# Order of matmuls in a six-layer cross network: two column groups interleaved over four pairs of PSUM banks, remainder rows of neighbouring groups placed side by side

## Chip and metric

One core of a Trainium2 chip. The metric is device microseconds of one execution. "Before" is an already tuned kernel.

## The reference

```python
B, F, D, L = 1024, 26, 32, 6          # Din = 26*32 = 832 columns
def reference(x0, ws, bs):            # x0 [1024, 832], ws [6, 832, 832], bs [6, 832], all bf16
    x = x0
    for l in range(6):
        x = x0 * (x @ ws[l] + bs[l]) + x
    return x
```

832 = 6 x 128 + 64. Each layer therefore has six full blocks of 128 and a remainder of 64, both in the rows that are contracted and in the columns that come out.

## The kernel before: what matters here

The batch lies along the free dimension, in two halves `c` of 512. A "group" is one block of output columns `j` of one layer (`KT = 7` groups: six full blocks and the remainder columns `KFULL`). TensorE works one group at a time, and alternates between two pairs of PSUM banks (PSUM is the memory into which matmuls add up their results). The loop, shortened:

```python
for g, (l, j) in enumerate(groups):          # layers 0-4: j = 0..6; layer 5: 6, 0..5
    s = g % 2                                # two bank pairs
    if g >= 2: eng.wait_ge(sem_act, group_first_item[g - 1])   # group g-2 evicted
    for kt in range(KT):                     # 6 full row blocks, then the 64 remainder rows
        for c in range(NCH):
            if first_in_layer: eng.wait_ge(sem_dve, ...)       # x tile kt, c of the layer before
            ...
            # kt < KFULL : rows 0:128                                    -> shape 128 x 128
            # kt == KFULL: rows 0:64 for c = 0, rows 64:128 for c = 1    -> shape  64 x 128
            # j == KFULL : columns 0:64 for c = 0, 64:128 for c = 1      -> 128 x 64, and 64 x 64
            mm = eng.matmul(ps_y[s][c], lhsT=w_sb[rows, l, kt, cols], rhs=xin[...],
                            start=(kt == 0), stop=(kt == KT - 1), tile_position=(trow, tcol))
```

The 64-row matmuls of the two halves run next to each other in the array; so do the 64-column ones. Two such matmuls are called a pair below. ScalarE evicts each half, that is, copies it out of PSUM with the bias added, to `t_buf`; VectorE multiplies by x0 and adds x. The add of item f is issued after the multiply of item f + 1. In layer 5 each finished block, except 4 and 5, is transposed by DMA (issued by SyncE) and stored by GpSimd; blocks 4 and 5 are transposed on TensorE and stored at the very end by SyncE and ScalarE, 256 KB each.

## Time and profile before

| | before |
|---|---|
| time, first measurement | 139.18 us (138.56 to 139.33, 4 runs) |
| span of the profiled run | 137.5 us, granted TensorE clock 0.993 |
| layers 1 to 4, start to start | 19.86 us each |
| layer 5, start to its last pair of matmuls | 20.24 us |
| last pair to the end of the span | 7.53 us |

Starts are those of the first weight load of a layer in the trace. The lines of the page and the views on which the argument rests are in the prediction below. How to read them: in these traces a weight load (PEld) between matmuls of one shape runs hidden under the matmul before it, so its row in the timeline goes on without a break. Where the shape changes, the row breaks; the bracket at the end of a row gives the idle time before it. A stay in the 64-row shape is called a visit or a cluster below, the time from the last pair to the end of the span the tail, and the time that one matmul or one pair takes up, 0.216 us, a slot.

### The profile page before, as it was taken

Reading aid. Unit: us, or ns where it says so; the run is one execution under the profiler, and the core shown is the slowest. Engines: PE = TensorE matmul, PEld = TensorE weight load, DVE = VectorE, ACT = ScalarE, POOL = GpSimd, SP = SyncE. Lnnn points to the kernel's source line nnn. Section 1 sums busy time; section 2 is a strip of 40 time slices with the busy share of each in tenths; the row PEclk is TensorE's granted clock in tenths of the full one; section 3 lists DMA queues with packets and bytes.
Section 4 is the critical chain, followed back from the end, with each engine's and each line's share of the span. In section 5 each row is a group of like instructions: output and inputs, shape, how many; then the busy total and the mean of one; then the engine's idle time right before and its main releaser. Section 6 shows DMA issues by size and latency. Waiting matters only on the chain.

```text
span 137.5 us, 1881 instructions
## 1 busy us (share of the span) xinstructions
PE 128.2 (93%) x692; PEld 55.5 (40%) x704; DVE 61.7 (45%) x164; ACT 52.0 (38%) x82; POOL 5.8 (4%) x12
## 2 busy tenths in 40 slices
PE   5989999999999999999999999999999989999930
PEld 5973333334443343333443343434433334433410
DVE  0180345553455453454473444463445552554570
ACT  0006544353433353333443344424444333333440
POOL 3000000000000000000000000000000000031520
PEclk9999999999999999999999999999999999999997
DMA  3998760000930001910003900005600000256757
GB/s 91 348 218 280 218 216 0 0 0 5 290 144 2 0 0 21 374 45 0 0 0 90 343 1 5 0 0 173 261 0 0 0 7 0 38 114 153 177 142 214
DMA packets 17016, 13.65 MB, mean 99 GB/s; under 512 B 7242, under 2 KB 16720, under 8 KB 17008
## 3 DMA queue, kind: packets, MB, share of 16 engines
q1 hardware_dynamic: 14192, 10.83, 26.5%
q10 hardware_dynamic: 2416, 1.52, 4.0%
q0 software_dynamic: 400, 1.19, 3.0%
q8 instruction: 5, 0.08, 0.3%
q14 instruction: 3, 0.02, 0.1%
HBM read 10.66 MB, written 1.70 MB: 90 GB/s over the span
## 4 chain that ended last, share of the span: by engine, by line
PE 80%; DMA 7%; ACTq 3%; ACT 3%; DVE 2%; issue 2%; POOL 1%; SPq 0%; DVEq 0%
PE ps_y L466 80%; DMA x_nat<-in_x_dram 4%; DMA o_sb<-xT_b 3%; ACT t_buf L519 2%; DVE u_buf L564 1%; ACTq L263 1%; ACT L498 1%; POOL out_dram L303 1%; DVE xT_a L578 1%; ACTq L245 1%; ACTq L248 0%; ACTq L256 0%; ACTq L260 0%; ACT x0T L506 0%; SPq L278 0%
## 5 line engine op out<-in xcount | busy, mean ns | idle before, releaser
L519 ACT ACTIVATE t_buf<-ps_y,bias_T 128x512 bf16<-128x512 f32 x77 | 49.1, 683 | 69.0 <-PE ps_y L466 69.0
L564 DVE TENSOR_TENSOR u_buf<-t_buf,x0T 128x512 bf16<-128x512 bf16 x76 | 32.1, 422 | 64.4 <-ACT t_buf L519 64.4
L466 PE MATMUL ps_y<-xT_a,w_sb 128*128 128x512 bf16 (+3 forms) x288 | 59.8, 382 | 0.7 <-DVE xT_a L578 0.3
L466 PE MATMUL ps_y<-xT_b,w_sb 128*128 128x512 bf16 (+2 forms) x192 | 39.5, 382 | 0.3 <-issue 0.2
L466 PEld LDWEIGHTS ps_y<-xT_a,w_sb 128*128 128x128 bf16 (+3 forms) x294 | 23.6, 99 | 36.7 <-issue 13.2
L466 PEld LDWEIGHTS ps_y<-xT_b,w_sb 128*128 128x128 bf16 (+3 forms) x196 | 15.7, 99 | 24.1 <-issue 9.1
L466 PE MATMUL ps_y<-x0T,w_sb 128*128 128x512 bf16 (+3 forms) x96 | 19.7, 382 | 0.5 <-ACT x0T L506 0.3
L578 DVE TENSOR_TENSOR xT_b<-u_buf,xT_a 128x512 bf16<-128x512 bf16 x37 | 15.2, 417 | 0.0
L466 PEld LDWEIGHTS ps_y<-x0T,w_sb 128*128 128x128 bf16 (+3 forms) x98 | 7.8, 99 | 12.2 <-issue 3.9
L578 DVE TENSOR_TENSOR xT_a<-u_buf,xT_b 128x512 bf16<-128x512 bf16 x26 | 10.7, 418 | 0.0
L303 POOL DMA_DIRECT2D out_dram<-o_sb x5 | 4.5, 895 | 127.3 <-DMA o_sb<-xT_b 127.3
L498 ACT ACT_TABLE_LOAD x1 | 1.3, 1283 | 11.1 <-issue 11.1
L360 PE MATMUL ps_x<-ident 128*128 128x128 bf16 x36 | 4.0, 313 | 1.5 <-POOL ident L336 1.5
L578 DVE TENSOR_TENSOR xT_a<-u_buf,x0T 128x512 bf16<-128x512 bf16 x13 | 5.3, 417 | 0.0
L360 PEld LDWEIGHTS ps_x<-ident 128*128 128x128 bf16 x36 | 3.8, 149 | 1.5 <-POOL ident L336 1.5
L554 DVE COPY x0T<-ps_t 128x1024 bf16<-128x1024 bf16 x2 | 1.3, 686 | 6.3 <-PE ps_t L393 6.3
L554 DVE COPY x0T<-ps_y 128x1024 bf16<-128x1024 bf16 x4 | 2.6, 686 | 0.4 <-PE ps_y L393 0.3
L393 PE MATMUL ps_y<-ident,x_nat 128*128 128x128 bf16 x32 | 2.1, 220 | 0.5 <-DMA x_nat<-in_x_dram 0.5
L393 PEld LDWEIGHTS ps_y<-ident,x_nat 128*128 128x128 bf16 x32 | 1.8, 98 | 0.7 <-DMA x_nat<-in_x_dram 0.7
L484 PE MATMUL ps_t<-ident,xT_b 128*128 128x128 bf16 x8 | 0.8, 222 | 1.3 <-DVE xT_b L612 0.9
L393 PE MATMUL ps_t<-ident,x_nat 128*128 128x128 bf16 x16 | 1.3, 251 | 0.0
L393 PEld LDWEIGHTS ps_t<-ident,x_nat 128*128 128x128 bf16 x16 | 1.3, 120 | 0.0
(26 smaller groups left out, 10.1 us busy)
## 6 DMA issues: line engine op xcount, KB each, us to landing
w_sb<-in_ws_dram SPq DMA_DIRECT2D x10, 624.0 KB, 4.7
w_sb<-in_ws_dram SPq DMA_DIRECT2D x10, 104.0 KB, 5.1
x_nat<-in_x_dram SPq DMA_DIRECT2D x2, 512.0 KB, 4.6
out_dram<-o_sb POOLq DMA_DIRECT2D x4, 256.0 KB, 3.8
w_sb<-in_ws_dram ACTq DMA_DIRECT2D x1, 864.0 KB, 5.0
x_nat<-in_x_dram SPq DMA_DIRECT2D x1, 640.0 KB, 6.7
out_dram<-o_sb SPq DMA_DIRECT2D x1, 256.0 KB, 2.3
out_dram<-o_sb ACTq DMA_DIRECT2D x1, 256.0 KB, 2.6
```

Source lines behind the costliest of these rows:

```text
L245: eng.dma_start(w_sb[0:REM, 0, KFULL, c0:c1], ws[0, RB:D, c0:c1]).then_inc(sem_w0blk[j], 16)
L263: eng.dma_start(w_sb[REM : 2 * REM, 0, KFULL, c0:D], ws[0, RB:D, c0:D]).then_inc(sem_w[0], 16)
L303: eng.dma_start(out[:, c0:c1].rearrange("(bo bi) f -> bi bo f", bi=P), o_sb[:, :, c0:c1],).then_inc(sem_out, 16)
L360: eng.matmul(ps_x[:, 0:P], lhsT=ident[:, :], rhs=ident[:, :], start=True, stop=True)
L393: eng.matmul(pt[:, bt * P : (bt + 1) * P], lhsT=x0_nat[:, bt, kt * P : (kt + 1) * P], rhs=ident[:, :], is_transpose=True,).then_inc(sem_tr, 1)
L466: mm = eng.matmul(o_ap, lhsT=lhsT, rhs=rhs, start=(kt == kt_first), stop=(kt == kt_last), tile_position=(trow, tcol), skip_group_check=(tc ...
L484: eng.matmul(pt[:, bb * P : (bb + 1) * P], lhsT=xf[:, j, bt * P : (bt + 1) * P], rhs=ident[:, :], is_transpose=True,).then_inc(sem_otr, 1)
L498: eng.activation(bias_T[:, 0:NB_COLS], ps_x[:, 0:NB_COLS], ACT_F.Copy).then_inc(sem_bc, 1)
L519: eng.activation(t_buf[:, slot, :], src, ACT_F.Identity, bias=bias_col(l, j), scale=1.0,).then_inc(sem_act, 1)
L554: eng.tensor_copy(x0T[:, kt, 0:ncol], tr_bank[kt][:, 0:ncol]).then_inc(sem_cp_v, 1)
L564: eng.tensor_tensor(u_buf[:, us, :], t_buf[:, slot, :], x0T[rows, tile, cols], ALU.mult,).then_inc(sem_u, 1)
L578: eng.tensor_tensor(xout[rows, tile, cols], u_buf[:, us, :], xin[rows, tile, cols], ALU.add,).then_inc(sem_dve, 1)
```

## The change

Its intent: fewer changes between full and 64-row matmuls, more slack in PSUM, and no start of a layer with a short group. It has four parts, in the diff as follows.

```diff
+ # (1) "SG": two groups interleaved, kt outermost; (2) third field 1: remainder rows first
+        if l == 0:
+            ph = [("G", [0]), ("G", [1], 1), ("SG", [2, 3]), ("SG", [4, 5]), ("G", [KFULL])]
+        elif l < L - 1:
+            ph = [("SG", [0, 1]), ("SG", [2, 3], 1), ("SG", [4, 5]), ("G", [KFULL])]
+        else:                       # (4) remainder columns no longer first in layer 5
+            ph = [("SG", [0, 1]), ("G", [KFULL]), ("G", [2], 1), ("G", [3])]
+            ph += [("G", [4], 1), ("G", [5])]
-        order = list(range(KT)) if l < L - 1 else [KFULL] + list(range(KFULL))
 ...
-        ps_y = [[ps_y0, ps_y1], [ps_y2, ps_y3]]
+        BP = [(ps_t0, ps_t1), (ps_y0, ps_y1), (ps_y2, ps_y3), (ps_b, ps_x)]   # (3), bitcasts cut
+        def bank_pair(g): return BP[g % NBP]
 ...
-                if g >= 2:
-                    eng.wait_ge(sem_act, group_first_item[g - 1])
+                if g >= NBP:
+                    eng.wait_ge(sem_act, group_first_item[g - NBP + 1])
 ...
+                        ktl = list(range(KT)) if not rem_first else [KFULL] + list(range(KFULL))
+                        for kt in ktl:
+                            for g, j in zip(gs, js):
+                                for c in range(NCH):
+                                    mm = eng.matmul(...)
 ...
+                    if l == L - 1 and (j, c) in [(KFULL, None)]:
+                        emit_add(f)         # VectorE: no deferral for the remainder columns
```

More of the change, by code (lines that the diff above doesn't have):

```diff
@@ L35, in bass_standalone__dcn_v2_cross__recsys_kernel @@
     UB_R = 4
+    SGW = 2
+    assert KFULL % SGW == 0
+    layer_phases = []
+    for l in range(L):
+        if l == 0:
[5 more added lines that the diff above has]
+            ph += [("G", [4], 1), ("G", [5])]
+        ph = [(p + (0,))[:3] for p in ph]
+        layer_phases.append(ph)
     groups = []
     for l in range(L):
-        order = list(range(KT)) if l < L - 1 else [KFULL] + list(range(KFULL))
-        for j in order:
-            groups.append((l, j))
+        for kind, js, _rf in layer_phases[l]:
+            for j in js:
+                groups.append((l, j))
     NG = len(groups)
@@ L58, in bass_standalone__dcn_v2_cross__recsys_kernel @@
     group_first_item.append(NF)
-    layer_first_item = [group_first_item[group_pos[(l, (0 if l < L - 1 else KFULL))]] for l in range(L)]
+    layer_first_item = [group_first_item[l * KT] for l in range(L)]
     layer_first_item.append(NF)
@@ L139, in bass_standalone__dcn_v2_cross__recsys_kernel @@
         block = es.enter_context(nc.Block(no_gpsimd_drain=True))
-        ps_y = [[ps_y0, ps_y1], [ps_y2, ps_y3]]
-        ps_t = [ps_t0, ps_t1]
         xT_bufs = [xT_a, xT_b]
@@ L166, in bass_standalone__dcn_v2_cross__recsys_kernel, with bank_pair @@
                 cp_wait.append((False, n_cp_v))
-        assert NPE == 2
-        s_last = (NG - 1) % 2
+        BP = [
+            (ps_t0[:, :].bitcast(FP32), ps_t1[:, :].bitcast(FP32)),
+            (ps_y0[:, :], ps_y1[:, :]),
+            (ps_y2[:, :], ps_y3[:, :]),
+            (ps_b[:, :], ps_x[:, :]),
+        ]
+        NBP = len(BP)
+        def bank_pair(g):
+            return BP[g % NBP]
+        assert NPE == 2 and NBP >= 4
         def piece_psum(k, c):
             if k == len(pe_groups) - 1:
-                return ps_t[c][:, 0 : HBT * P]
-            return ps_y[1 - s_last][c][:, :].bitcast(BF16)[:, 0 : HBT * P]
+                return bank_pair(NG - 3)[c].bitcast(BF16)[:, 0 : HBT * P]
+            return bank_pair(NG - 2)[c].bitcast(BF16)[:, 0 : HBT * P]
         def final_store(eng, c, sem):
@@ L416, in wait_x0T_copy @@
                 eng.wait_ge(sem_cp_a if on_act else sem_cp_v, cnt)
-            tr_bank_users_g0 = [kt for kt in range(KT) if tr_bank[kt].tensor.name in ("ps_y0", "ps_y1")]
-            for g, (l, j) in enumerate(groups):
-                xin = x_in(l)
-                s = g % 2
-                first_in_layer = group_first_item[g] == layer_first_item[l]
-                if g >= 2:
-                    eng.wait_ge(sem_act, group_first_item[g - 1])
-                kt_order = list(range(KT))
-                kt_first, kt_last = kt_order[0], kt_order[-1]
-                if True:
-                    for kt in kt_order:
-                        for c in range(NCH):
-                            if first_in_layer:
-                                if l == 0:
-                                    if c == 0:
-                                        if kt == kt_first:
-                                            for ku in tr_bank_users_g0:
-                                                wait_x0T_copy(ku)
-                                        wait_x0T_copy(kt)
-                                else:
-                                    eng.wait_ge(sem_dve, item_index[(l - 1, kt, c)] + 1)
-                                if kt == kt_first and c == 0 and l > 0:
-                                    eng.wait_ge(sem_w[l], W_SEM_TOTAL)
-                            if l == 0 and kt == kt_first and c == 0:
-                                if j < W0_NBLK:
-                                    eng.wait_ge(sem_w0blk[j], W0_BLK_TOTAL)
-                                elif j == W0_NBLK:
-                                    eng.wait_ge(sem_w[0], W0_REST_TOTAL)
-                            if kt < KFULL:
-                                rows = slice(0, P)
-                                rhs = xin[:, kt, c * NW : (c + 1) * NW]
-                                trow = 0
-                            elif c == 0:
-                                rows = slice(0, REM)
-                                rhs = xin[0:REM, KFULL, 0:NW]
-                                trow = 0
-                            else:
-                                rows = slice(REM, 2 * REM)
-                                rhs = xin[REM : 2 * REM, KFULL, 0:NW]
-                                trow = REM
-                            if j < KFULL:
-                                lhsT = w_sb[rows, l, kt, j * P : (j + 1) * P]
-                                o_ap = ps_y[s][c][:, :]
-                                tcol = 0
-                            else:
-                                lhsT = w_sb[rows, l, kt, RB:D]
-                                o_ap = ps_y[s][0][c * REM : (c + 1) * REM, :]
-                                tcol = c * REM
-                            mm = eng.matmul(
-                                o_ap,
-                                lhsT=lhsT,
-                                rhs=rhs,
-                                start=(kt == kt_first),
-                                stop=(kt == kt_last),
-                                tile_position=(trow, tcol),
-                                skip_group_check=(tcol != 0),
-                            )
-                            if kt == kt_last and (j < KFULL or c == NCH - 1):
-                                mm.then_inc(sem_mm, 1)
@@ new lines, in _, with pre_group_waits @@
+            tr_bank_names = [tr_bank[kt].tensor.name for kt in range(KT)]
+            def pre_group_waits(g):
+                l, j = groups[g]
+                if g >= NBP:
+                    eng.wait_ge(sem_act, group_first_item[g - NBP + 1])
+                else:
+                    for bnk in bank_pair(g):
+                        name = bnk.tensor.name
+                        for kt in range(KT):
+                            if tr_bank_names[kt] == name:
+                                wait_x0T_copy(kt)
+                        if name == "ps_x":
+                            eng.wait_ge(sem_bc, 1)
@@ new lines, in mm_operands @@
+            def mm_operands(l, j, kt, c, g):
+                xin = x_in(l)
+                if kt < KFULL:
+                    rows = slice(0, P)
+                    rhs = xin[:, kt, c * NW : (c + 1) * NW]
+                    trow = 0
+                elif c == 0:
+                    rows = slice(0, REM)
+                    rhs = xin[0:REM, KFULL, 0:NW]
+                    trow = 0
+                else:
+                    rows = slice(REM, 2 * REM)
+                    rhs = xin[REM : 2 * REM, KFULL, 0:NW]
+                    trow = REM
+                if j < KFULL:
+                    lhsT = w_sb[rows, l, kt, j * P : (j + 1) * P]
+                    o_ap = bank_pair(g)[c]
+                    tcol = 0
+                else:
+                    lhsT = w_sb[rows, l, kt, RB:D]
+                    o_ap = bank_pair(g)[0][c * REM : (c + 1) * REM, :]
+                    tcol = c * REM
+                return o_ap, lhsT, rhs, trow, tcol
@@ new lines, in tile_wait, with weights_wait @@
+            def tile_wait(l, kt, c):
+                if l == 0:
+                    wait_x0T_copy(kt)
+                else:
+                    eng.wait_ge(sem_dve, item_index[(l - 1, kt, c)] + 1)
+            def weights_wait(l, js):
+                if l > 0:
+                    eng.wait_ge(sem_w[l], W_SEM_TOTAL)
+                else:
+                    for j in js:
+                        if j < W0_NBLK:
+                            eng.wait_ge(sem_w0blk[j], W0_BLK_TOTAL)
+                    if max(js) >= W0_NBLK:
+                        eng.wait_ge(sem_w[0], W0_REST_TOTAL)
@@ new lines, in _ @@
+            for l in range(L):
+                first_phase = True
+                for kind, js, rem_first in layer_phases[l]:
+                    gs = [group_pos[(l, j)] for j in js]
+                    if kind == "G":
+                        g = gs[0]
+                        j = js[0]
+                        pre_group_waits(g)
+                        ktl = list(range(KT)) if not rem_first else [KFULL] + list(range(KFULL))
+                        for kt in ktl:
+                            for c in range(NCH):
+                                if first_phase:
+                                    if kt == KFULL or j == KFULL:
+                                        if c == 0:
+                                            for cc in range(NCH):
+                                                tile_wait(l, kt, cc)
+                                    else:
+                                        tile_wait(l, kt, c)
+                                if kt == ktl[0] and c == 0 and (first_phase or l == 0):
+                                    weights_wait(l, js)
+                                o_ap, lhsT, rhs, trow, tcol = mm_operands(l, j, kt, c, g)
+                                mm = eng.matmul(
+                                    o_ap,
+                                    lhsT=lhsT,
+                                    rhs=rhs,
+                                    start=(kt == ktl[0]),
+                                    stop=(kt == ktl[-1]),
+                                    tile_position=(trow, tcol),
+                                    skip_group_check=True,
+                                )
+                                if kt == ktl[-1] and (j < KFULL or c == NCH - 1):
+                                    mm.then_inc(sem_mm, 1)
+                    else:
+                        assert all(j < KFULL for j in js)
+                        for g in gs:
+                            pre_group_waits(g)
+                        assert not (first_phase and rem_first)
+                        if l == 0 and rem_first:
+                            weights_wait(l, js)
+                        ktl = list(range(KT)) if not rem_first else [KFULL] + list(range(KFULL))
+                        for kt in ktl:
+                            if first_phase:
+                                for cc in range(NCH):
+                                    tile_wait(l, kt, cc)
+                            if kt == 0 and (first_phase or l == 0) and not rem_first:
+                                weights_wait(l, js)
+                            for g, j in zip(gs, js):
+                                for c in range(NCH):
+                                    o_ap, lhsT, rhs, trow, tcol = mm_operands(l, j, kt, c, g)
+                                    mm = eng.matmul(
+                                        o_ap,
+                                        lhsT=lhsT,
+                                        rhs=rhs,
+                                        start=(kt == ktl[0]),
+                                        stop=(kt == ktl[-1]),
+                                        tile_position=(trow, tcol),
+                                        skip_group_check=True,
+                                    )
+                                    if kt == ktl[-1]:
+                                        mm.then_inc(sem_mm, 1)
+                    first_phase = False
@@ L512, in _ @@
                 g = group_pos[(l, j)]
-                s = g % 2
                 slot = f % TB_R
@@ L517, in _ @@
                 eng.wait_ge(sem_mm, f + 1)
-                src = ps_y[s][c][:, :] if j < KFULL else ps_y[s][0][:, :]
+                src = bank_pair(g)[c] if j < KFULL else bank_pair(g)[0]
                 eng.activation(
@@ L589, in _ @@
                     f1 = NF - 2
+                pend = None
                 for f in range(f0, f1):
                     emit_mult(f)
-                    if f > f0:
-                        emit_add(f - 1)
-                emit_add(f1 - 1)
+                    if pend is not None:
+                        emit_add(pend)
+                    pend = f
+                    _, j, c = items[f]
+                    if l == L - 1 and (j, c) in [(KFULL, None)]:
+                        emit_add(f)
+                        pend = None
+                if pend is not None:
+                    emit_add(pend)
             xin5 = x_in(L - 1)
@@ L604, in _ @@
                 out=u_buf[:, us1, :],
-                in0=ps_y[s_last][1][:, :],
+                in0=bank_pair(NG - 1)[1],
                 scalar=bias_col(L - 1, J_LAST),
```

## The prediction

> **What bounds the kernel now.** I read the page first, then its chain of work, then the timeline of the weight loads (PEld).
>
> ```profile
> PE 128.2 (93%) x692; PEld 55.5 (40%) x704; DVE 61.7 (45%) x164; ACT 52.0 (38%) x82; POOL 5.8 (4%) x12
> ...
> PE   5989999999999999999999999999999989999930
> PEld 5973333334443343333443343434433334433410
> DVE  0180345553455453454473444463445552554570
> ...
> PE 80%; DMA 7%; ACTq 3%; ACT 3%; DVE 2%; issue 2%; POOL 1%; SPq 0%; DVEq 0%
> ```
>
> TensorE is busy from slice 3 to slice 37 and holds 80% of the chain that ended last; VectorE and ScalarE are under half busy. So there is next to no waiting to remove, and the question is whether a "busy" TensorE does useful work all the time. A busy digit can't tell, because modelled ends of matmuls overlap the next start. Starts can. A weight load that can't be hoisted stands within 4 ns of its matmul, so the PEld timeline marks the places where the array changes its shape; here it is in layer 0:
>
> ```profile
> 16.17 0.10 PEld L466 LDWEIGHTS ps_y<-x0T,w_sb 64*128 64x128 bf16 x2 [0.42 <-issue]
> 16.49 2.27 PEld L466 LDWEIGHTS ps_y<-x0T,w_sb 128*128 128x128 bf16 x12 [0.23 <-issue]
> 19.18 0.10 PEld L466 LDWEIGHTS ps_y<-x0T,w_sb 64*128 64x128 bf16 x2 [0.42 <-issue]
> 19.51 2.27 PEld L466 LDWEIGHTS ps_y<-x0T,w_sb 128*128 128x128 bf16 x12 [0.23 <-issue]
> 22.20 0.10 PEld L466 LDWEIGHTS ps_y<-x0T,w_sb 64*128 64x128 bf16 x2 [0.42 <-issue]
> ```
>
> One column group is twelve full matmuls (six row blocks, two batch halves) and one pair of 64-row matmuls for the remainder of 64 rows, which run side by side (their starts are 4 ns apart in the single records). The period is (22.20 - 16.17) / 2 = 3.015 us; 3.019 from the single matmul records. Full matmuls start every 0.216 us. Thirteen such slots are 2.807 us, so **0.21 us of each group is neither a matmul slot nor a wait**: it is the way into and out of the 64-row shape. From the starts of the single matmuls: the last full one to the 64-row pair 0.312 instead of 0.216 (0.096 extra); the pair to the next full one 0.323, and that one takes 0.226 (0.117 extra together). Measured in the same way at the end of each layer: 64-row pair to the 128x64 shape of the remainder columns 0.127 extra; 128x64 to 64x64 0.096; 64x64 back to full 0.129, or 0.142 where a 128x64 group follows (layer 4 to 5).
>
> Only one real wait stands in the matmul stream after layer 0 has begun, in the last layer, which begins with the short remainder-column group:
>
> ```profile
> 109.42 0.11 PEld L466 LDWEIGHTS ps_y<-xT_b,w_sb 64*64 64x64 bf16 x2 [0.41 <-issue]
> 109.75 1.00 PEld L466 LDWEIGHTS ps_y<-xT_a,w_sb 128*64 128x64 bf16 x11 [0.23 <-issue]
> 111.53 0.11 PEld L466 LDWEIGHTS ps_y<-xT_a,w_sb 128*64 128x64 bf16 x1 [0.77 <-DVE xT_a L578]
> 111.86 0.11 PEld L466 LDWEIGHTS ps_y<-xT_a,w_sb 64*64 64x64 bf16 x2 [0.23 <-DVE xT_a L578]
> 112.20 0.55 PEld L466 LDWEIGHTS ps_y<-xT_a,w_sb 128*128 128x128 bf16 x4 [0.23 <-issue]
> ```
>
> This group takes 112.20 - 109.75 = 2.45 us; the same group in the other layers takes 1.75 (48.42 to 50.17 in the same view). So 0.70 us is waiting for VectorE's add on the previous layer's last tiles. In the other layers no first group waits (30.316 to 33.335 is again 3.019); the 0.4 us holes that the chain shows there, such as 41.33 to 41.76, are records that are missing, since the count of twelve comes out one short each time.
>
> The end, from the chain in order of time:
>
> ```profile
> 128.25 0.42 DVE u_buf L564
> 128.67 0.11 DVE xT_b L578
> 128.78 0.14 issue
> 128.92 0.11 DVE u_buf L564
> 129.03 3.99 DMA o_sb<-xT_b
> 133.02 0.28 issue
> 133.31 0.89 POOL out_dram L303
> ```
>
> The last matmul pair starts at 129.99; the span ends 7.5 us later. Bound there is not that pair's own output (its store has landed at 136.17) but column block 3: its last add waits, by program order, behind the first multiply of block 4, then transposes by DMA, then is stored and lands at 137.13.
>
> **What the Trainium skill says.** "TensorEngine Tiling (Array Packing)", Key Properties: "Changing tiling mode (not just tile) drains the TensorE". The trace agrees, at 0.10 to 0.14 us a change. "TensorE: Matmul & The Clock Gate", the section on 56 ns against 53.3: a warm matmul of 512 columns takes 512/2.4 GHz plus about 2.5 ns, 215.7 ns; the trace has 216, so no slot can become shorter. The same page, The mechanism: a weight load overlaps running matmuls only when its row group differs. The trace shows more: in the 128x128 and 128x64 shapes loads of about 0.1 us are hidden and slots stay at 0.216 and 0.216. For two 64-row pairs in succession, which the change makes for the first time, no run shows it. "TensorEngine Tiling", Gotcha 1: row tiles must not be in the same PSUM bank at once; the two halves of a pair keep separate banks in the change.
>
> **The change part by part.** It (1) handles two column groups together, row block outermost; (2) lets alternate phases begin with the remainder rows, so that their 64-row pairs touch those that ended the phase before; (3) uses four pairs of PSUM banks in place of two, which (1) and (2) need; (4) in layer 5 puts blocks 0 and 1 ahead of the remainder columns. Matmul slots, evictions, VectorE work and bytes stay the same in number. Weight loads too: each matmul keeps its own, hidden as now.
>
> Shape changes before. Layers 0 to 3: five inner clusters at 0.096 + 0.117 = 0.213, the sixth into the remainder columns 0.096 + 0.127, then 0.096 + 0.129: 1.065 + 0.223 + 0.225 = 1.513 us. Layer 4: 1.526. Layer 5: 0.225 + 1.065 + 0.096 = 1.386. In all 4 x 1.513 + 1.526 + 1.386 = 8.96 us.
>
> After. Layer 0: clusters {block 0, block 1} and {2, 3} at 0.213, {4, 5} 0.223, remainder columns 0.225: 0.874. Layers 1 to 4: one inner cluster {0, 1, 2, 3}, {4, 5} at 0.223, 0.225: 0.661 each. Layer 5: {0, 1} into the remainder columns 0.223, into 64x64 0.096, from there into block 2's 64-row pair about 0.12 (not seen so far; an estimate between the 0.096 and 0.142 above), out 0.117, {3, 4} 0.213, into block 5's pair 0.096: 0.865. In all 0.874 + 4 x 0.661 + 0.865 = 4.38 us. **Gain 4.58 us**, all of it in TensorE's stream, so on the path.
>
> The wait in layer 5: 5.4 us of work on blocks 0 and 1 now hide the adds: block 5's tiles are needed 20 slots (4.3 us) into the layer instead of 1.1. Gain 0.70 us.
>
> The end: block 4 now ends with full matmuls and its first half is out earlier, 2.64 instead of 2.53 us before the last pair's start, which brings block 3's add 0.1 us forward against the end. The rest stays: 0.1 us. At the head nothing moves: the first group still waits 0.32 us at its remainder pair (13.15) for ScalarE's copy, and the weights of block 1 (landed 10.34, now wanted 13.37) and of the rest (landed 14.27, wanted 16.28) are there.
>
> Sum: 4.58 + 0.70 + 0.1 = 5.4 us; 139.18 - 5.4 = **133.8 us**.
>
> **The rivals.** (a) *Bunched results make new waits.* Four halves now finish within 0.43 us instead of two. ScalarE issues evictions 0.585 us apart, VectorE two operations at 0.336 each, so a bunch of four is through about 4 us after its first pair starts. Next layer's first phase needs block 4's banks free 2.29 us after that start (two pairs' slots, then 1.75 of remainder columns) and has them at 0.485 + 0.585 + 0.68 = 1.75; it needs block 5's tiles at 6.6 and has them at about 4.6. It fits, by 0.5 and 2 us. Were it to miss by 0.5 us at five boundaries: 136.3. Chance about 7%. (b) *The second 64-row pair's load is not hidden.* Then each of the 21 pairs that now follow another pair costs some 0.1 us again: 2.1 us, 135.9. The 128x64 shape, where loads are hidden, speaks against it. Chance about 10%. (c) *The end takes back the gain*: the DMA transposes of blocks 2 and 3 come 2.7 instead of 3.0 us apart and share the queues with stores; a transpose took 3.0 to 4.0 us in this trace. Half a us either way. (d) Weights of the next layer are asked for after 5.6 instead of 3.0 us of a layer and land 6.7 us later, well within 19 us: hidden as now.
>
> **Range and chances.** The middle is the sum. Downwards only the end (a 3 us transpose) and the unseen shape change move it: 133.0. Upwards rival (c), some of (a) or half of (b): 135.4. Two per cent faster is 136.4; (a) or (b) alone stay under it, both together pass it. Faster 0.93, same 0.06, slower 0.01.
>
> **What would show it.** Right: PEld timeline of layers 1 to 4 with two 64-row clusters per layer instead of six, of eight and four loads; layers of 19.0 us instead of 19.86; pairs inside a cluster 0.216 apart (0.31 would be rival b); no wait on VectorE at layer 5's start; a tail after the last pair still of 7.4 us. Wrong: waits of TensorE on ScalarE or VectorE at layer starts, or a clock granted lower than the present 0.993.

## The result

| | before | after |
|---|---|---|
| time, median | 139.0 us (138.46 to 139.48, 16 runs) | 133.9 us (133.22 to 134.52, 11 runs) |
| ratio | | 0.963, 95% interval 0.9609 to 0.9651 |
| profiled span | 137.5 us | 131.5 us |
| layers 0, 1 to 4, 5 | 20.18, 4 x 19.86, 20.24 | 19.22, 4 x 19.01, 19.01 |
| last pair to the end | 7.53 us | 7.55 us |

A ratio is the mean time of one kernel's runs over the mean of the other's of the same rounds, so it is not quite the ratio of the medians. The two profiled spans differ by 6.0 us, the medians by 5.1. The profiled execution before was one of its slower ones: layer 0 waited 0.32 us there for a copy, and began 0.44 us later than in the profile after. In the run of this kernel with earlier adds (below), whose head is the same, layer 0 took 19.86. With that value the matmul stream from the start of layer 0 to the last pair is 5 x 19.86 + 20.24 = 119.54 before and 19.22 + 5 x 19.01 = 114.27 after: 5.27 us less.

The page of the changed kernel:

```profile
PE 123.0 (93%) x692; PEld 55.8 (42%) x704; DVE 59.9 (46%) x164; ACT 49.7 (38%) x82; POOL 5.8 (4%) x12
...
PE   5989999999999999999999999999999999999920
...
DVE  0280433556166274338091628190725370934660
ACT  0006515171427090616170724451642623534430
```

TensorE has the same number of matmuls and the same busy share; the share says nothing of the gain. VectorE and ScalarE were level before; now they swing between 0 and 9 tenths, since results come four halves at a time. TensorE does not wait for them: from the start of layer 0 to the last pair the totals of its waits name neither.

The timeline of weight loads after, from the start of layer 1 to that of layer 2; it answers to the one of layer 0 in the prediction:

```profile
28.91 0.10 PEld L543 LDWEIGHTS ps_b<-xT_a,w_sb 128*128 128x128 bf16 x1 [0.23 <-issue]
...
34.20 0.09 PEld L543 LDWEIGHTS ps_b<-xT_a,w_sb 64*128 64x128 bf16 x1 [0.42 <-issue]
34.20 0.09 PEld L543 LDWEIGHTS ps_x<-xT_a,w_sb 64*128 64x128 bf16 x1
34.21 0.10 PEld L543 LDWEIGHTS ps_t<-xT_a,w_sb 64*128 64x128 bf16 x2
34.43 0.31 PEld L543 LDWEIGHTS ps_y<-xT_a,w_sb 64*128 64x128 bf16 x4
35.17 4.86 PEld L543 LDWEIGHTS ps_y<-xT_a,w_sb 128*128 128x128 bf16 x24 [0.42 <-issue]
...
45.63 0.09 PEld L543 LDWEIGHTS ps_b<-xT_a,w_sb 64*128 64x128 bf16 x1 [0.42 <-issue]
...
46.17 1.00 PEld L515 LDWEIGHTS ps_y<-xT_a,w_sb 128*64 128x64 bf16 x12 [0.42 <-issue]
...
47.92 0.11 PEld L543 LDWEIGHTS ps_y<-xT_b,w_sb 128*128 128x128 bf16 x2 [0.23 <-issue]
```

Eight 64-row loads stand together at 34.20, and the next full load comes at 35.17: four pairs for one visit to the 64-row shape. The second cluster, at 45.63, serves blocks 4 and 5. There are two visits in a layer where there were six, and the layer takes 47.92 - 28.91 = 19.01 us.

The start of layer 5, which answers to the lines with the wait for VectorE:

```profile
110.25 0.10 PEld L543 LDWEIGHTS ps_t<-xT_a,w_sb 64*128 64x128 bf16 x2
110.78 1.00 PEld L515 LDWEIGHTS ps_y<-xT_a,w_sb 128*64 128x64 bf16 x12 [0.42 <-issue]
112.19 0.11 PEld L515 LDWEIGHTS ps_y<-xT_a,w_sb 64*64 64x64 bf16 x2 [0.41 <-issue]
112.53 0.10 PEld L515 LDWEIGHTS ps_y<-xT_a,w_sb 64*128 64x128 bf16 x2 [0.23 <-issue]
112.85 0.55 PEld L515 LDWEIGHTS ps_y<-xT_a,w_sb 128*128 128x128 bf16 x4 [0.23 <-issue]
```

All idle time here ends by "issue", none by VectorE. The remainder columns take 112.53 - 110.78 = 1.75 us, as in any other layer.

The end did not go as predicted. The transfers by kind in the last part of the trace (operation, count, KB each, median us from issue to landing), before:

```profile
out_dram<-o_sb SPq DMA_DIRECT2D x1, 256.0 KB, 2.3
out_dram<-o_sb ACTq DMA_DIRECT2D x1, 256.0 KB, 2.6
```

and after:

```profile
out_dram<-o_sb SPq DMA_DIRECT2D x1, 256.0 KB, 3.3
out_dram<-o_sb ACTq DMA_DIRECT2D x1, 256.0 KB, 3.5
```

The last of the chain is now ScalarE's store, not GpSimd's. Block 3's transpose took 3.08 us instead of 3.99, so its store was issued 2.3 us after the last pair instead of 3.3. It then ran ahead of the two final stores, which landed 1.0 and 0.9 us later after the last pair than before.

### The profile page after: what moved, and what is told of

Read it like the earlier page. It is cut to its first block, busy times and chain, and to the rows that moved or that the text cites. A ratio compares the mean times of both kernels' runs of the same rounds, so it can differ in the third digit from the quotient of the medians.

```text
span 131.5 us, 1929 instructions
## 1 busy us (share of the span) xinstructions
PE 123.0 (93%) x692; PEld 55.8 (42%) x704; DVE 59.9 (46%) x164; ACT 49.7 (38%) x82; POOL 5.8 (4%) x12
## 4 chain that ended last, share of the span: by engine, by line
PE 86%; DMA 5%; DVE 3%; issue 1%; SPq 1%; ACT 1%; DVEq 0%; ACTq 0%
PE ps_y L543 30%; PE ps_t L543 17%; PE ps_y L515 11%; PE ps_b L543 9%; PE ps_x L543 8%; PE ps_t L515 6%; DMA x_nat<-in_x_dram 5%; PE ps_b L515 2%; PE ps_x L515 1%; DVE u_buf L641 1%; PE ps_y L414 1%; SPq L299 1%; DVE u_buf L687 1%; ACT t_buf L596 1%; DVE xT_b L655 0%
## 5 line engine op out<-in xcount | busy, mean ns | idle before, releaser
L596 ACT ACTIVATE t_buf<-ps_y,bias_T 128x512 bf16<-128x512 f32 x37 | 23.2, 689 | 31.8 <-PE ps_y L543 23.9
L543 PE MATMUL ps_y<-xT_b,w_sb 128*128 128x512 bf16 (+1 forms) x81 | 22.8, 379 | 0.2
L596 ACT ACTIVATE t_buf<-ps_t,bias_T 128x512 bf16<-128x512 f32 x21 | 13.4, 688 | 16.9 <-PE ps_t L543 14.6
L543 PE MATMUL ps_y<-xT_a,w_sb 128*128 128x512 bf16 (+1 forms) x81 | 17.3, 379 | 0.2
L543 PE MATMUL ps_t<-xT_a,w_sb 128*128 128x512 bf16 (+1 forms) x54 | 15.4, 379 | 0.1
L543 PE MATMUL ps_t<-xT_b,w_sb 128*128 128x512 bf16 (+1 forms) x41 | 11.7, 380 | 0.1
L543 PE MATMUL ps_b<-xT_a,w_sb 128*128 128x512 bf16 (+1 forms) x28 | 10.7, 381 | 0.0
L543 PE MATMUL ps_x<-xT_a,w_sb 128*128 128x512 bf16 (+1 forms) x28 | 10.6, 380 | 0.0
L515 PE MATMUL ps_y<-xT_a,w_sb 128*64 128x512 bf16 (+3 forms) x56 | 9.7, 383 | 0.0
L543 PE MATMUL ps_b<-xT_b,w_sb 128*128 128x512 bf16 (+1 forms) x21 | 8.0, 379 | 0.0
```

Of the source, the lines that this page charges most:

```text
L515: mm = eng.matmul(o_ap, lhsT=lhsT, rhs=rhs, start=(kt == ktl[0]), stop=(kt == ktl[-1]), tile_position=(trow, tcol), skip_group_check=True,)
L543: mm = eng.matmul(o_ap, lhsT=lhsT, rhs=rhs, start=(kt == ktl[0]), stop=(kt == ktl[-1]), tile_position=(trow, tcol), skip_group_check=True,)
L596: eng.activation(t_buf[:, slot, :], src, ACT_F.Identity, bias=bias_col(l, j), scale=1.0,).then_inc(sem_act, 1)
```

## The experiments

Every experiment was timed in five rounds against the kernel before, whose median over these rounds was 138.82 to 138.85 us. "Layers" are read as in the table above. The diffs of the orders are put in short form. The runs with parts of the change are made from the changed kernel, so they keep the rest of its code too, such as the undeferred add of the remainder columns.

### Part 3 alone: four pairs of banks

```diff
+ ph = [("G", [j]) for j in order]     # order as before: 0..6; layer 5: 6, 0..5
```

> Part 3 alone: four pairs of PSUM banks, with the old order of groups and rows. My theory (the gain is fewer shape changes of the array plus one removed wait): the shape changes and the wait in layer 5 stay, so 139.0 us, within 0.3 of before, and layers of 19.86 us. Rival (TensorE was held back at group ends by PSUM banks that were not yet free): most of the gain of 5.1 us comes here, 134 to 136.

Measured: 138.94 us, ratio 1.0014 (0.9991 to 1.0038); layers 19.86, layer 5 20.33. No gain from banks: TensorE had not been waiting for them. That the other parts need the four pairs is argued from the code; none was run with two.

### Parts 3 and 4: order in layer 5

```diff
- layer 5: G 6, G 0, G 1, G 2, G 3, G 4, G 5
+ layer 5: G 0, G 1, G 6, G 2, G 3, G 4, G 5
```

> Parts 3 and 4: as the one before, and in layer 5 the remainder columns go behind blocks 0 and 1, one group at a time. My theory: only the wait of 0.70 us at the start of layer 5 goes and the number of shape changes stays: 138.3 us, with no wait on VectorE there. Rival (the wait is hidden by the tail, which ends later in any case): 139.0.

Measured: 137.94 us, ratio 0.9946 (0.9921 to 0.9971), 0.75 us less; layer 5 19.54, 0.70 less than before. The wait was on the path, and its worth is its length.

### Parts 2 and 3: neighbouring remainder rows without interleaving

```diff
+ layers 0-4: G 0, G 1 (rem first), G 2, G 3 (rem first), G 4, G 5 (rem first), G 6
+ layer 5:    G 6, G 0, G 1 (rem first), G 2, G 3 (rem first), G 4, G 5
```

> Parts 2 and 3 without interleaving: one group at a time, but blocks 1, 3, 5 (1 and 3 in layer 5) begin with the remainder rows, so that 64-row pairs of two groups touch; layer 5 in the old order. My theory: shape changes cost 0.98 us in layers 0 to 4 (three clusters at 0.213, full into 128x64 taken as 0.12, 0.225) and 0.96 in layer 5, 5.9 in place of 8.96; gain 3.0 us, the wait in layer 5 stays: 136.0 us, layers 1 to 3 of 19.3 us. Rival (the gain is interleaving of two groups, whatever it does for the array): 139.0.

Measured: 135.91 us, ratio 0.9794 (0.9767 to 0.982); layers 0 to 4 19.33. Six visits became three without any interleaving, and 2.9 us were gained. So the gain follows the number of shape changes. The new change from full straight to 128x64 fits the 0.12 that was taken for it: first steps of 0.309 and 0.237 us where 0.216 and 0.213 would be without it.

### Parts 1, 3 and 4: interleaving without neighbouring remainder rows

```diff
- ("G", [1], 1)   ("SG", [2, 3], 1)   ("G", [2], 1)   ("G", [4], 1)
+ ("G", [1])      ("SG", [2, 3])      ("G", [2])      ("G", [4])
```

> Parts 1, 3 and 4 without part 2: groups interleaved in twos as in the change, but every phase ends with its remainder rows. My theory: 1.087 us of shape changes in layer 0, 0.874 in layers 1 to 4, 1.18 in layer 5, 5.77 in place of 8.96, and the wait of 0.70 gone: gain 3.9 us, 135.1 us, layers 1 to 4 of 19.2 us, 1.3 us above the whole change. Rival (interleaving alone makes the gain): 133.9.

Measured: 135.02 us, ratio 0.9731 (0.9706 to 0.9756); layers 1 to 4 19.22. Interleaving is worth what it merges: two pairs per visit, three visits a layer.

### The change with part 4 undone

```diff
- layer 5: SG 0 1, G 6, G 2 (rem first), G 3, G 4 (rem first), G 5
+ layer 5: G 6, G 0, G 1 (rem first), G 2, G 3 (rem first), G 4, G 5
```

> The change with part 4 undone: layer 5 begins with the remainder columns again, then blocks 0 to 5 one at a time with 1 and 3 beginning with their remainder rows. My theory: the wait at the start of layer 5 comes back and is longer than the old 0.70 us, since layer 4 now hands over four halves at once: its last add is at about 5.05 us after the last 64-row cluster starts, and the 64x64 pair that needs it would be due at 3.7, so 1.4 us; and 0.1 us of shape changes: 1.5 us over the whole change, 135.4. Rival (the old wait of 0.70 simply comes back): 134.7.

Measured: 135.68 us, ratio 0.9768 (0.9735 to 0.9802); layer 5 20.61. The weight loads at the start of layer 5:

```profile
105.58 0.57 PEld L515 LDWEIGHTS ps_b<-xT_a,w_sb 128*64 128x64 bf16 x8 [0.23 <-issue]
106.78 0.14 PEld L515 LDWEIGHTS ps_b<-xT_a,w_sb 128*64 128x64 bf16 x2 [0.63 <-DVE xT_a L655]
108.12 0.14 PEld L515 LDWEIGHTS ps_b<-xT_a,w_sb 128*64 128x64 bf16 x2 [1.20 <-DVE xT_a L655]
...
108.83 0.11 PEld L515 LDWEIGHTS ps_t<-xT_a,w_sb 128*128 128x128 bf16 x2 [0.23 <-issue]
```

The remainder columns take 108.83 - 105.58 = 3.25 us instead of 1.75: a wait of 1.50 us, twice the old one, so the rival fell. The time itself is 1.8 us above the change's, but three of its six executions have 2.9 to 3.1 us between span and time, where nearly all others of this study have 1.7 to 2.1; by the spans (medians 133.35 and 131.85) it is 1.5 us, as expected. Interleaving at the end of a layer hands VectorE four halves at once, and a short group at the start of the next can't cover them. Parts 1 and 4 belong together.

### The price of a shape change, by taking the shape away

Wrong result on purpose (relative error 0.049): both halves' remainder rows are read by full-height matmuls.

```diff
-  elif c == 0: rows, rhs, trow = slice(0, REM), xin[0:REM, KFULL, 0:NW], 0
-  else:        rows, rhs, trow = slice(REM, 2*REM), xin[REM:2*REM, KFULL, 0:NW], REM
+  else:        rows, rhs, trow = slice(0, P), xin[:, KFULL, 0:NW], 0
```

> Wrong result on purpose. The kernel before, with the remainder rows done as two full 128-row matmuls one after the other (both halves' rows are read, so the sums are wrong) in place of one pair of 64-row ones side by side. A group then has 14 full slots and no shape change inside. My theory (0.21 us of each group is the change of shape): 14 x 0.216 = 3.02 us, as long as before, so 139.0 within 0.4 us although 36 more slots are used. Rival (the 0.21 us belongs to the end of a group, its semaphore or the change of PSUM banks): 3.23 us a group, 36 x 0.21 = 7.6 us more, 146.6.

Measured: 138.99 us, ratio 1.0015 (0.999 to 1.0039). Weight loads of layer 2 in this run:

```profile
50.38 17.81 PEld L462 LDWEIGHTS ps_y<-xT_b,w_sb 128*128 128x128 bf16 x84 [0.41 <-ACT t_buf L515]
68.61 1.22 PEld L462 LDWEIGHTS ps_y<-xT_b,w_sb 128*64 128x64 bf16 x14 [0.42 <-issue]
```

84 loads of six groups go through without one break. Their matmuls start from 50.382 to 68.306: 83 steps of 0.216 us, over five group ends and their bank changes. The end of a group costs nothing, so the 0.21 us belonged to the shape. And 36 more slots cost no time: before the change, running the two 64-row matmuls side by side saved one slot and paid one slot's worth of shape changes for it.

### The end of the kernel before, with earlier adds

```diff
                 emit_mult(f)
                 ...
+                if l == L - 1 and c in (None, 1):
+                    emit_add(f)            # not behind the next block's multiply
```

> The kernel before, with one thing changed at the end: in the last layer the add of a block's second half is issued right after its multiply, not behind the next block's first multiply. The DMA transpose of block 3 then starts 2.3 us earlier. Theory A (of the prediction: block 3's transpose and store end the kernel before): the end is then set by the last pair's own store, which landed 0.97 us earlier than block 3's; gain 1.0 to 1.4 us, 137.6 to 138.0. Theory B (the three stores at the end share the DMA engines, and the last one issued lands at the same time whatever the order): under 0.4 us.

Measured: 137.93 us, ratio 0.9951 (0.9911 to 0.9992), 0.9 us less in the medians and 0.7 by the ratio; the tail after the last pair went from 7.53 to 6.56 us in the profile. Theory A holds for the kernel before, at slightly less than its range: block 3's late add did set its end.

### The same at the end of the change

> The change, with the same edit at the end of it. In the profile of the change the last chain is the last pair's own store, landing 3.55 us after its issue, in company with block 3's store issued 1.25 us before it. Theory A (what is issued late shares the engines with block 3's store and is slowed by it): with block 3's store issued about 1.7 us earlier, the last store lands in 2.6 to 3.0 us, gain 0.5 to 1.0 us, 132.9 to 133.4. Theory B (two stores of 256 KB alone fill that time): under 0.3 us, 133.6 to 133.9.

Measured: 133.78 us, ratio 0.9644 (0.9618 to 0.9669), no gain over the change's 0.963. In the profile block 3's transpose was issued 1.8 us earlier against the last pair, as intended, but took 4.4 us instead of 3.1, so its store was issued only 0.5 us earlier. The condition of theory A, a store 1.7 us earlier, was thus not met. As far as the store did move, the profile goes A's way: the last store landed in 3.02 us instead of 3.54, and the tail was 7.03 us. The times don't show it: the other three executions have spans of 131.6 to 132.1 us, the change a median of 131.85. Whether this edit gains half a microsecond stays open.

That a neighbour slows the final stores is seen in other traces too. Block 3's store was issued 2.7 us before SyncE's final store in the old kernel with earlier adds, 1.3 in the last run below, 1.1 here and 0.7 in the change; SyncE's store then took 2.3, 2.6, 2.8 and 3.35 us, ScalarE's 2.55, 2.8, 3.0 and 3.5. In the kernel before it was issued 0.35 us after SyncE's, which took 2.3, and ScalarE's 2.6.

### Blocks 0 and 1 stored together, meant to make fewer packets

```diff
-  store block 0 (256 KB, rows of 256 bytes); store block 1
+  store blocks 0 and 1 as one transfer (512 KB, rows of 512 bytes), after both transposes
```

> The change, with blocks 0 and 1 of the output stored as one transfer of 512-byte rows in place of two of 256-byte rows (they finish together in the change). Nothing else moves. It tells whether the number of small packets in the last 14 us is what holds the end: theory C (yes): the last stores land 2.6 to 3.0 us after their issue instead of 3.55, gain 0.4 to 0.8 us, 133.1 to 133.5. Theory B (the end is filled by the stores issued last alone, earlier traffic is done by then): under 0.2 us, 133.7 to 133.9.

Measured: 134.28 us, ratio 0.9667 (0.9632 to 0.9702); tail 8.06. With the earlier adds as well:

> The change with both edits of the end: the earlier adds, and blocks 0 and 1 stored together. In the run with the earlier adds alone the transposes of blocks 2 and 3 took 4.4 to 4.5 us in company with the stores of blocks 0, 1 and the remainder, and block 3's store began only 0.4 us earlier than in the change. Theory C (fewer packets in that company): the transpose of block 3 takes 3.0 to 3.5 us, the tail after the last matmul pair shrinks from 7.0 to about 6.6 us as in the old kernel with earlier adds, 132.9 to 133.3 us. Theory B: the transposes stay above 4 us, 133.5 to 133.8.

Measured: 134.71 us, ratio 0.9687 (0.9652 to 0.9721); tail 8.79. Two of its transfers from 112 us on:

```profile
out_dram<-o_sb POOLq DMA_DIRECT2D x1, 512.0 KB, 7.7
...
out_dram<-o_sb POOLq DMA_DIRECT2D x1, 128.0 KB, 7.0
```

The gains that theory C forecast did not come; both runs are slower than their counterparts, with intervals that overlap. But the edit did not test theory C. The packets from 112 us on, in the change and in the run with both edits:

```profile
DMA packets 6224, 2.88 MB, mean 103 GB/s; under 512 B 4912, under 2 KB 5936, under 8 KB 6224
DMA packets 6208, 2.88 MB, mean 103 GB/s; under 512 B 4896, under 2 KB 5920, under 8 KB 6208
```

Rows of twice the length took away 16 packets of 6224, and the other run has the same count. So whether small packets hold the end stays untested. What the edit did change is the company: in the run with both edits the joint store starts later and runs together with the remainder's store and block 2's transpose; all three landed within 0.7 us of each other after 7 to 8 us, where in the kernel before a full block's transpose took 3 to 4 with a store or two under way. That this pile-up made the longer tails is likely, not shown. Why such a company is that slow, no run here shows.

### Earlier adds, and output spread out again

```diff
  layer 5, over the run with earlier adds:
-  SG 0 1, G 6, G 2 (rem first), ...
+  G 0, G 1 (rem first), G 6, G 2 (rem first), ...
```

> A try at a version better than both. The change with the earlier adds of the end, and layer 5 no longer interleaves blocks 0 and 1: block 0, block 1 beginning with its remainder rows, remainder columns, then as in the change. Block 0's output is then out 2.6 us earlier and the transposes and stores of the end lie further apart, as they did in the old kernel with earlier adds. Matmul stream: layer 5 pays 0.974 in place of 0.865 us for shape changes (full into 128x64 taken as 0.12) and, from the times of the adds in the profile of the change, some 0.1 us of waiting for layer 4's last two adds; 0.2 us more. Theory D (what slows the end is transposes and stores that overlap): tail 6.6 us instead of 7.5, in all 0.7 us less than the change, 133.0 to 133.4. If overlap is not it: the tail stays at 7.0 to 7.5 and the time is 133.8 to 134.1.

Measured: 133.14 us (132.88 to 133.62, 6 runs), ratio 0.959 (0.9562 to 0.9618). Layer 5 took 19.33 us, 0.32 more than in the change (0.2 expected); the tail was 6.84 us. The sum, 0.4 us less, is what the profile shows; the medians show 0.7 to 0.8. It is the fastest kernel, ahead of both; but its interval and the change's (0.9609 to 0.9651) still touch, so its lead over the change is likely rather than settled. The tail lies between theory D's 6.6 and the rival's 7.0. Against the run with earlier adds alone (tail 7.03, layer 5 19.00) the profiles give nothing: spans of 131.1 us each. The times are 0.6 us apart. So theory D isn't settled either, and as it was not run without the earlier adds, how the two edits share the gain is open.

## Why the prediction was right

Predicted 133.8 us, 133.0 to 135.4; measured 133.9. By its steps:

- **Shape changes, 4.58 us.** Right, and shown: by the layers (19.01 as forecast for 1 to 4), by the two runs that do one half of the merging each (3.0 us expected, and 3.9 with the wait's share; 2.9 and 3.7 measured by the ratios), and by the run without the 64-row shape. The unseen change from 64x64 to 64-row, estimated at 0.12, shows as 112.53 - 112.19 = 0.34 us against a slot of 0.216: 0.12.
- **The wait in layer 5, 0.70 us.** Right: 0.75 by itself. (The work that hides the adds is 26 slots and their shape changes, 5.83 us in the trace, and not 5.4; nothing hangs on it.) Stream in all: 5.28 predicted, 5.27 in the traces.
- **Rival (a), bunched results.** No new wait in the change. The forecast of late adds was good enough to size the wait that appears when part 4 is undone (1.4 expected, 1.50 measured).
- **Rival (b), a second 64-row pair whose load is not hidden.** False: single records inside a cluster start 0.223, 0.211 and 0.213 us apart.
- **The head.** "At the head nothing moves" was half right. The wait of 0.32 us for ScalarE's copy, which the prediction also left out where it says that only one real wait stands in the stream, is absent in the profile after. But it is absent too in the kernel before with earlier adds, and the run without neighbouring rows waited about 0.4 us there: so its absence can't be put down to the change.
- **Banks.** The halves of a 64-row pair have separate banks, as said. The two 64x64 matmuls don't: in both kernels the code puts them in the two partition halves of one bank. They start 3 to 4 ns apart, and the results are correct.
- **The end, 0.1 us.** The step that failed, within the range. Block 3's transpose was issued 0.1 us earlier against the last pair, as forecast. But the prediction said block 3's store would still end the kernel. It ends before the final stores, which it now slows; the tail was 7.55 us instead of 7.4. This was rival (c) in kind: what one transfer gained, its neighbours gave back.

The time fell by 5.1 us in the medians, where 5.4 were forecast; the stream fell by 5.27. The interval of the ratio is 4.85 to 5.43 us, so the 0.1 to 0.2 us between them are noise as far as can be told. That the time itself was met within 0.1 us is partly luck: the sum started from a first measurement of 139.18 us, 0.2 above the later median. The clock, which the prediction named as a sign of being wrong, was granted at 0.986 in the profile after, below 0.993; but the timed executions of both kernels have 0.984 to 0.996, and slots stayed at 0.216 us.

## What to carry to other kernels

A TensorE that is busy all the time can still lose time at changes of the array's shape; look for breaks in the timeline of weight loads, and count them. Put matmuls of the same shape next to each other, across groups if PSUM has room, and check that what follows is long enough to hide the results that then come in bunches. An edit that finishes output earlier can lose its gain where the transfers that it moves meet others, as the same edit gained 0.7 to 0.9 us in the kernel before and nothing measurable in the change: read issue and landing of each one, not only who ended last. And check in the trace that an edit changed what it was meant to change, such as the number of packets, before a theory is judged by it.

## What the Trainium skill lacked or had wrong

- "TensorEngine Tiling (Array Packing)", Key Properties, says that a change of mode drains the array but gives no figure: here 0.096 us into a 64-row shape from full, 0.117 back, 0.21 us for a visit, 0.10 to 0.14 for the others. That makes a lone 64-row pair as slow as two full matmuls in turn (138.99 against 138.83 us), which the page's "Up to 2x" doesn't lead one to expect.
- "TensorE: Matmul & The Clock Gate", The mechanism, says in its list of what overlaps that a weight load overlaps running matmuls only when the row group differs. The paragraph above that list also names loads into a background weight buffer, so "only" is too narrow by the page itself; the prediction read the list alone. Here loads are hidden within the same row group too: 0.216 us a slot with loads of 0.098 us, and 0.211 to 0.223 us between 64-row pairs.
- The same page, Back-to-back issue gap, gives about 131 ns a matmul of 512 columns as the sustained figure and calls some 216 an over-count. Here an unbroken stream of 84 ran at 216 ns, as the page's own formula has it.
- "DMA: Bandwidth & Descriptors", in its rules for kernel authors, says that a transpose next to ordinary DMAs needs nothing. That is about correct results; it lacks the time: a full block's transpose took 3.0 to 4.0 us in the kernel before and 8.1 us with a 512 KB and a 128 KB store beside it.
